# Re-planned tiles, banks and order of a two-branch kernel (head-wise linear attention beside an SSM convolution)

## The chip, the core and the metric

The kernel runs as one program on one core of a Trainium2 chip. The metric is the device time of one execution in microseconds (us). Engines are named as the profile names them: PE is TensorE (PEld its weight loads), DVE is VectorE, ACT is ScalarE, POOL is GpSimd, SP is SyncE, which here only issues DMAs.

## The reference

Two independent parts are computed and put side by side, 448 columns each, in bf16.

```python
# A: x 2048x448, 16 heads of 28
qkv = x @ wqkv
pq, pk = q @ w_phi, k @ w_phi                     # per head
phi = concat(softmax(p), softmax(-p))             # for q and for k
kv, z = phi_k^T v, sum of phi_k                   # per head
o = (phi_q kv) / (phi_q z + 1e-6);  a = o @ wo
# B: u 2048x448, 256 states for each column
dt = exp(log_dt)[:, None];  dA = dt * (A_re + 1j * A_im)
K[d, l] = real(sum_n C[d, n] * exp(dA[d, n] * l) * dt[d] * B[d, n])
b = causal_convolution(u, K) + u * Dskip
```

## The kernel before

**The A part.** x is loaded in four blocks of 512 rows and transposed on TensorE (`flip_x`, eight banks of transposes and eight evictions). `fold_weights` multiplies w_phi into the q and k weights. `key_side` runs over eight pairs of 128 tokens: projections, two Exp for each block (scale +1 and -1), a transposing DMA of the Exp tile on SP's queue (L600), matmuls with a 0/1 table that sum over heads, a reciprocal on VectorE (L187), the product VR and the key-value matmuls. `query_side` runs four times on 512 tokens: projection, Exp, a small normalisation on VectorE, a round trip through DRAM (SCd) that spreads it over partitions, two products, the output matmuls.

**The B part.** `to_states` turns A, B and C, which have the 448 columns on partitions, into tiles with 128 states on partitions (two halves of 256), by a matmul with a diagonal of dt; ScalarE's Exp and Sin then give the powers PW of exp(dA). The positions l, as bf16 holds them, are sums of a low position (48 rows) and a high one (16 rows). The 448 columns are done in four quarters (`qt`) of 112, each with 224 elements on each partition (112 columns, two state halves). For each quarter `rotations` (Sin), `dampings` (Exp), `damp` and `far` make the low table W, `hi_tables` the high table U, and `build_k` contracts both over the states with 448 small matmuls in 4 column groups. `scatter_k` rearranges K through DRAM. `signal_spectrum` and `kernel_spectrum` are matmuls with transform tables, `conv` multiplies the spectra on VectorE and transforms back (`inverse`), and stores.

**What sets the order.** No loop does. Each operation is recorded (`Prog.add`) and then issued in the order of the list ORDER, 1104 operations written out by hand or by a planner; each engine runs its own in that order, and waits for the others by semaphores. PSUM banks come from a second list, SLOTS. SBUF is one tile of 212,800 bytes on each partition, cut at offsets that are constants in the code (`oW`, `oT`, ...), some used twice. Copies are bound to an engine in the code: `acopy` (L193) on ScalarE, `vcopy` (L180) on VectorE, `smul` (L174) on VectorE; all other VectorE products and sums are L162, all Exp, Sin and Square are L190, all matmuls L201, transposes L211, all DMAs L216.

**Around the change.** u is loaded twice: even rows with 896-byte runs on SP (`rep_rows`), odd rows in reverse order, one row of 896 bytes for each partition and step, on POOL (`pair_rows`); VectorE then forms sum and difference (`ab`). The raw A, B and C tiles are loaded with 512-byte runs, `(j p) n -> p j n`. POOL issues 22 DMAs: eight of u, four of w_phi, the head mask, Dskip, wo, the head-sum table, the two halves of the inverse table GI, and the four SUd tiles of the convolutions. In ORDER, five of the eight key pairs stand ahead of `damp` of quarter 0.

Of the kernel before, what the change touches and what calls it, by code (L numbers as in the profile page):

```python
# [15 lines left out]

D_MODEL = 448
D_HEAD = 28
# [28 lines left out]
def _dft_tables():  # L47
# [24 lines left out]
    pid = np.zeros((128, 9, 128))  # L72
    for i, p in enumerate(ODD + [-1]):
        pid[np.arange(128), i, np.arange(128)] = p
    hm = np.zeros((112, 4, D_HEAD + 1))
# [7 lines left out]
class Prog:  # L83


    def __init__(self):
        self.ops = []
        self.jobs = []

    def take(self, kind, *slots):  # L90
        self.jobs.append((kind, slots, len(self.ops)))
        return SLOTS[len(self.jobs) - 1] if SLOTS else slots
# [13 lines left out]
def kernel(  # L106
# [26 lines left out]
    sbuf = sb_pool.tile([128, 212800 // 2], BF16, name="sbuf")  # L133
# [4 lines left out]
    def sb(off, shape, dtype=BF16):  # L138
        size = int(np.prod(shape[1:])) * (4 if dtype == F32 else 2)
        v = sbuf[0:shape[0], off // 2:(off + size) // 2]  # L140
        if dtype == F32:
            v = v.bitcast(F32)
        names = "abcdefg"[:len(shape) - 1]
        if len(names) > 1:
            v = v.rearrange(f"p ({' '.join(names)}) -> p {' '.join(names)}",
                            **{n: s for n, s in zip(names[1:], shape[2:])})
        return v
# [25 lines left out]
    def smul(o, a, s):  # L173
        prog.add("V", lambda: nc.vector.tensor_scalar_mul(o, a, s))  # L174

# [3 lines left out]
    def vcopy(o, a):  # L179
        prog.add("V", lambda: nc.vector.tensor_copy(o, a))  # L180

    def low(fn):
        with nc.allow_low_precision(reason="bf16 softmax weights, as in the reference"):
            fn()

    def recip(o, a):
        prog.add("V", lambda: low(lambda: nc.vector.reciprocal(o, a)))  # L187
# [4 lines left out]
    def acopy(o, a):  # L192
        prog.add("A", lambda: nc.scalar.copy(o, a))  # L193
# [20 lines left out]
    def dma(eng, o, i):  # L214
        e = {"S": nc.sync, "AD": nc.scalar, "G": nc.gpsimd}[eng]
        prog.add(eng, lambda: e.dma_start(out=o, in_=i))  # L216

    oCB, oAT, oTH, oPW, oW, oT, oU, oTM, oSQ, oTS, oKT, oX = (
        3584, 7168, 10752, 14336, 95104, 32256, 46592, 75264, 82432, 86912, 92400, 139008)
    PID = sb(0, [128, 9, 128])  # L220
    ident = PID[:, 0, :]
    NEG = PID[:, 8, :]
    DSK = sb(2304, [128, D_MODEL])
    HM = sb(3200, [112, 4, D_HEAD + 1])
    K0 = sb(86016, [128, D_MODEL])
    bias_hp = sb(3440, [128, 1], F32)
    KVZ = sb(3456, [112, 2, 4, 4, 2])
    CB = sb(oCB, [128, 2, NCOL])
    AT = sb(oAT, [128, 2, NCOL])
    TH = sb(oTH, [128, 2, NCOL])  # L230
    PW = {k: sb(oPW + 3584 * i, [128, 2, NCOL]) for i, k in enumerate((32, 64, 128, 256, 512))}
    W = sb(oW, [128, 2, N_LO, QC])
    T = sb(oT, [128, 2, 16, QC])
    U = [sb(oU + 14336 * b, [128, N_HI, 2, QC]) for b in range(2)]
    TS = [sb(oTS + 2744 * b, [128, N_LO, 28]) for b in range(2)]
    KT = [sb(oKT + 1344 * b, [128, N_KT, 112]) for b in range(2)]
# [3 lines left out]
    xT = sb(oX, [112, 4, 2048])  # L240
    Wp = [sb(o, [112, 4, D_MODEL]) for o in (155392, 158976)]
    WV = sb(162560, [112, 4, D_MODEL])
    M = sb(158976, [112, 8, D_MODEL])
    wo = sb(166144, [112, 4, D_MODEL])
    G1 = sb(169728, [128, 2, 4, 512])
    raw = {nm: sb(oT + 2048 * i, [112, 4, SSM_N]) for i, nm in enumerate(("Are", "Aim", "Cre", "Bre", "Cim", "Bim"))}
    srcs = {"Are": B_A_re, "Aim": B_A_im, "Cre": B_C_re, "Bre": B_B_re, "Cim": B_C_im, "Bim": B_B_im}
    XS = [sb(o, [128, 4, D_MODEL]) for o in (oW + 10976, oW + 14560, oW + 18144, oW + 32928)]
    Wqk = sb(oW + 36512, [112, 4, 2 * D_MODEL])
    wT = sb(oTS, [112, 2, 4, D_MODEL])  # L250
    BD = sb(oTS + 7168, [112, 4, 112])
    DG = sb(oSQ + 1024, [112, 4, 112])
    DGN = sb(oSQ + 1920, [112, 4, 112])
    ldt = sb(oSQ + 2816, [4, 112])
    dtr = sb(oSQ + 3072, [4, 112])

    def load_raw(nm):
        dma("S", raw[nm], srcs[nm].rearrange("(j p) n -> p j n", p=112))
# [4 lines left out]
    wq3 = A_wqkv.rearrange("(j p) n -> p j n", p=112)  # L263
    dma("S", ldt, bass.AP(tensor=B_log_dt.tensor, offset=B_log_dt.offset, ap=[[112, 4], [1, 112]]))
    load_raw("Are")
    dma("S", PID, P_d)
    load_raw("Aim")
    load_x(0)
    for nm in ("Cre", "Bre", "Cim", "Bim"):
        load_raw(nm)  # L270
    for i in range(1, 4):
        load_x(i)
    dma("S", Wqk, wq3[:, :, 0:2 * D_MODEL])
    mset(BD, 0.0)
    for hh in range(4):
        dma("G", BD[28 * hh:28 * hh + 28, :, 28 * hh:28 * hh + 28], A_w_phi.rearrange("(c h) d f -> h d c f", h=4)[hh])
    prog.add("V", lambda: nc.vector.memset(bias_hp, PI / 2))

    def rep_rows(row, a):
        rs = u2.ap[0][0]  # L280
        return bass.AP(tensor=u2.tensor, offset=u2[row + 128 * (1 - a), 0].offset,
                       ap=[[2 * rs, 64], [256 * rs, 4], [1, D_MODEL]])

    def pair_rows(row, t):
        rs = u2.ap[0][0]
        return bass.AP(tensor=u2.tensor, offset=u2[row + 1023 - 128 - 256 * t, 0].offset,
                       ap=[[128 * rs, 2], [-2 * rs, 64], [1, D_MODEL]])

    ua = [sb(o, [128, 4, 2, D_MODEL]) for o in (oU, oW + 10976)]
    ab = [sb(o, [128, 2, 4, D_MODEL]) for o in (198336, oU + 14336)]  # L290

    def load_u(b):
        for a in range(2):
            dma("S", ua[b][64 * a:64 * a + 64, :, 0, :], rep_rows(1024 * b, a))
        for t in range(4):
            dma("G", ua[b][:, t, 1, :], pair_rows(1024 * b, t))

    load_u(0)
    dma("S", G1, G_d)
    dma("S", WV, wq3[:, :, 2 * D_MODEL:])  # L300

    af(dtr, ldt, ACT.Exp)
    (b_,) = prog.take("P", 6)
    dtp = bank16(b_, [112, 4])
    transposes([(dtp, dtr, PID[0:4, 0, 0:4])])
    mul(DG, PID[0:112, 0, 0:112].unsqueeze(1).to_broadcast([112, 4, 112]), dtp.unsqueeze(2).to_broadcast([112, 4, 112]))
    smul(DGN, DG, -1.0)
# [4 lines left out]
    def halves(v):  # L312
        return v.rearrange("p (b x) -> p b x", b=2)

    def to_states(bs, terms):
        items = []
        for j in range(4):
            for nch in range(2):
                at = (j % 2) * QC + nch * 56
                o = view(psum[:, bs[j // 2], at:at + 1], [112, 2], [14, 4], [1, 14])  # L320
                items += acc(o, [(t[:, j, 128 * nch:128 * nch + 128],
                                  d[:, j, :].rearrange("p (g c q) -> p c g q", c=2, q=14)) for t, d in terms])
        mms(items)

    bA, bT = prog.take("P", 0, 1), prog.take("P", 4, 5)
    for nm, b, dst in (("Are", bA, AT), ("Aim", bT, TH)):
        to_states(b, [(raw[nm], DG)])
        acopy(halves(dst[:, 0, :]), two(b))
        sub(halves(dst[:, 1, :]), two(b), halves(dst[:, 0, :]))
    prog.take("T", 0)  # L330
    prods = {}
    for i, (a, b) in enumerate((("Cre", "Bre"), ("Cim", "Bim"), ("Cre", "Bim"), ("Cim", "Bre"))):
        prods[a + b] = sb(oTM + 2048 * i, [112, 4, SSM_N])
# [3 lines left out]
    amp = [sb(o, [128, NCOL], F32) for o in (oW, oW + 3584, oW + 7168, oW + 21952)]  # L337
    cs = [sb(o, [128, 2, NCOL], F32) for o in (oW + 25536, oU + 7168)]
    qa = [sb(oU + 14336 + 7168 * i, [128, 2, NCOL], F32) for i in range(2)]
    s2 = sb(177920, [128, 2, NCOL], F32)  # L340
    CR = sb(166144, [128, 2, NCOL])
    PW[16] = sb(194752, [128, 2, NCOL])
    for n, k in enumerate(LOWP):
        af(halves(amp[n]), two(bA), ACT.Exp, scale=float(k))
    for part, terms in enumerate(([("CreBre", DG), ("CimBim", DGN)], [("CreBim", DG), ("CimBre", DG)])):
        bs = prog.take("P", *((6, 7), (2, 3))[part])
        to_states(bs, [(prods[n], d) for n, d in terms])
        acopy(halves(CR[:, part, :]), two(bs))
    ones = sb(186944, [128, 128])
    mset(ones, 2.0 ** -17)  # L350
    bs = prog.take("P", 0)
    mms([it for qt in range(4) for it in acc(
        view(psum[:, bs[0], 112 * qt:112 * qt + 1], [28, 4], [14, 2], [1, 14]),
        [(ones, view(CR[:, 0, QC * qt + 56 * nch:QC * qt + 56 * nch + 1], [14, 4], [112, 2], [1, 14]))
         for nch in range(2)])])
    acopy(K0, psum[:, bs[0], 0:D_MODEL])
    for n, k in enumerate(LOWP):
        c_ = cs[n % 2]
        af(halves(c_[:, 0, :]), two(bT), ACT.Sin, scale=float(k), bias=bias_hp)
        af(halves(c_[:, 1, :]), two(bT), ACT.Sin, scale=float(k))  # L360
        mul(PW[k] if k != 128 else qa[0], c_, amp[n].unsqueeze(1).to_broadcast([128, 2, NCOL]))
        if k == 128:
            acopy(PW[128], qa[0])
    cur = qa[0]
    for i, k in enumerate((256, 512)):
        af(s2, cur, ACT.Square)
        nxt = qa[(i + 1) % 2]
        sub(nxt[:, 0, :], s2[:, 0, :], s2[:, 1, :])
        stt(nxt[:, 1, :], cur[:, 0, :], 2.0, cur[:, 1, :], ALU.mult, ALU.mult)
        acopy(PW[k], nxt)  # L370
        cur = nxt
    prog.take("T", 0)
    TM = sb(oTM, [128, 2, 2, NCOL])
# [3 lines left out]

    def flip_x(i):
        for tp in range(2):
            p = bank16(*prog.take("P", 6 + tp), [112, 2, 4, 128])  # L380
# [541 lines left out]
```

## Time and profile before

| | us |
|---|---|
| median of 3 runs (lowest, highest) | 298.96 (296.89, 300.54) |
| span of the profiled execution, the only time it has | 299.6 |
| busy: DVE, PE, ACT, PEld, POOL | 244.4, 240.7, 203.4, 179.8, 16.0 |
| table loads of ACT | 13 of 1.28 each |
| bytes moved | 39.47 MB in 65,966 packets, mean 132 GB/s |
| mean granted clock of PE | 0.949 |

The page's busy times are unions: two instructions of an engine that overlap count once. A row of the table of groups gives the count, the busy time and the mean of one instruction, then the engine's idle time just before such instructions and what ended it. In the 40 slices one digit is the busy share of 7.5 us in tenths.

### The profile page before, as it was taken

The page shows a single profiled execution, that of the slowest core. Times are in us where ns is not written, and L with a number is a line of the kernel's source. Part 1 is how long each engine was busy: PE and PEld are TensorE (multiplying, and loading weights), DVE is VectorE, ACT ScalarE, POOL GpSimd, SP SyncE. Part 2 cuts the span into 40 slices and gives each one's busy share as a digit, 9 for nine tenths or more (in the row PEclk, how much of TensorE's full clock was granted, in tenths as well). Part 3 has the DMA queues.
Part 4 walks back from the last instruction along what each step waited for, and adds up shares of the span by engine and source line. Part 5 has one row for each costly group of instructions (what it writes and reads, how often), then busy time and mean ns, then how long its engine had stood idle before and what let it go on. Part 6 is the DMA issues. An engine that isn't in the chain of part 4 may idle for free. (4 is left out here: it accounts for less than half of the span.)

```text
span 299.6 us, 8829 instructions
## 1 busy us (share of the span) xinstructions
PE 240.7 (80%) x3877; PEld 179.8 (60%) x3877; DVE 244.4 (82%) x292; ACT 203.4 (68%) x343; POOL 16.0 (5%) x32
## 2 busy tenths in 40 slices
PE   1246997899469999986979996566998888999784
PEld 1245554567245567863447763466658678999784
DVE  4265995446249999997989999989899999999991
ACT  3749999599947999997199955871948611544431
POOL 8102201001000000000000001000000000000000
PEclk9999999999959999998695999777999999999999
DMA  7999387463804530045012533955879956667222
GB/s 161 239 231 194 79 246 145 64 181 67 107 10 122 122 64 4 6 136 104 3 61 58 85 79 85 331 146 109 227 255 293 301 136 176 147 184 135 46 65 63
DMA packets 65966, 39.47 MB, mean 132 GB/s; under 512 B 46616, under 2 KB 61992, under 8 KB 65544
## 3 DMA queue, kind: packets, MB, share of 16 engines
q1 hardware_dynamic: 62920, 31.57, 45.0%
q0 software_dynamic: 3008, 7.34, 8.9%
q8 instruction: 30, 0.49, 0.7%
q14 instruction: 8, 0.07, 0.1%
HBM read 26.36 MB, written 8.85 MB: 118 GB/s over the span
## 5 line engine op out<-in xcount | busy, mean ns | idle before, releaser
L201 PE MATMUL psum<-sbuf 128*16 128x48 bf16 (+9 forms) x3768 | 231.3, 258 | 39.1 <-DVE sbuf L162 11.1
L201 PEld LDWEIGHTS <-sbuf 128*16 128x16 bf16 (+4 forms) x3768 | 170.7, 109 | 98.3 <-issue 37.3
L162 DVE TENSOR_TENSOR sbuf<-sbuf 128x896 bf16<-128x896 bf16 (+13 forms) x227 | 216.7, 1002 | 12.1 <-DMA sbuf<-SCd 3.5
L193 ACT CAST sbuf<-psum 128x448 bf16<-128x448 f32 (+4 forms) x141 | 74.9, 581 | 70.6 <-PE psum L201 63.1
L190 ACT ACTIVATE sbuf<-psum 128x448 bf16<-128x448 f32 (+4 forms) x140 | 81.7, 674 | 13.2 <-DVE sbuf L162 7.5
L211 PE MATMUL psum<-sbuf 128*112 128x128 bf16 (+3 forms) x109 | 11.7, 267 | 16.2 <-DMA sbuf<-in_A_x_dram 7.2
L190 ACT ACTIVATE sbuf<-psum,sbuf 128x896 bf16<-128x896 f32 (+3 forms) x28 | 21.7, 812 | 0.0
L211 PEld LDWEIGHTS <-sbuf 128*112 128x112 bf16 (+3 forms) x109 | 10.0, 172 | 17.8 <-DMA sbuf<-in_A_x_dram 7.7
L187 DVE RECIPROCAL sbuf<-psum 128x64 bf16<-128x64 f32 x8 | 4.4, 555 | 19.4 <-PE psum L201 19.4
L190 ACT ACT_TABLE_LOAD x13 | 16.7, 1283 | 0.9 <-PEq L906 0.7
L190 ACT ACTIVATE sbuf<-sbuf 128x896 bf16<-128x896 bf16 (+3 forms) x13 | 11.6, 915 | 3.6 <-DVE sbuf L162 3.4
L180 DVE COPY sbuf<-psum 112x1024 bf16<-112x1024 bf16 (+2 forms) x16 | 7.3, 466 | 7.8 <-PE psum L211 6.6
L216 POOL DMA_DIRECT2D sbuf<-const x4 | 2.2, 556 | 126.0 <-PE psum L201 109.5
L162 DVE TENSOR_TENSOR sbuf<-psum,sbuf 128x128 f32<-128x128 f32 (+3 forms) x10 | 4.7, 491 | 3.8 <-ACT sbuf L193 3.8
L193 ACT COPY sbuf<-psum 112x896 bf16<-112x896 bf16 x5 | 4.5, 919 | 4.7 <-PE psum L211 4.7
L216 POOL DMA_DIRECT2D sbuf<-in_B_u_dram x8 | 6.6, 830 | 19.0 <-DMA sbuf<-in_B_B_re_dram 18.9
L174 DVE TENSOR_SCALAR sbuf<-sbuf 128x3584 bf16<-128x3584 bf16 (+4 forms) x11 | 6.5, 587 | 0.0
L216 POOL DMA_DIRECT2D sbuf<-SUd x4 | 2.1, 529 | 72.5 <-DVE sbuf L162 72.5
L193 ACT CAST sbuf<-sbuf 128x1792 bf16<-128x1792 f32 x3 | 5.1, 1703 | 0.0
L180 DVE COPY sbuf<-sbuf 128x448 bf16<-128x448 bf16 (+1 forms) x6 | 1.4, 238 | 3.1 <-DMA sbuf<-const 3.1
L177 DVE SCALAR_TENSOR_TENSOR sbuf<-sbuf 128x64 f32<-128x64 f32 (+1 forms) x6 | 3.0, 506 | 0.0
L196 POOL MEMSET sbuf<- 128x32 bf16 (+3 forms) x6 | 1.4, 261 | 24.7 <-PE psum L211 24.5
(12 smaller groups left out, 9.4 us busy)
## 6 DMA issues: line engine op xcount, KB each, us to landing
sbuf<-const SPq DMA_DIRECT2D x16, 384.0 KB, 3.2
SUd<-sbuf SPq DMA_DIRECT2D x8, 448.0 KB, 4.3
sbuf<-SCd SPq DMA_DIRECT2D x16, 224.0 KB
sbuf<-SUd POOLq DMA_DIRECT2D x4, 896.0 KB, 4.9
sbuf<-const POOLq DMA_DIRECT2D x2, 1024.0 KB, 7.9
sbuf<-in_A_x_dram SPq DMA_DIRECT2D x4, 448.0 KB
out_dram<-sbuf SPq DMA_DIRECT2D x4, 448.0 KB
sbuf<-in_B_u_dram SPq DMA_DIRECT2D x16, 112.0 KB, 4.0
```

The costliest lines, as they stand in the source:

```text
L162: prog.add("V", lambda: nc.vector.tensor_tensor(out=o, in0=a, in1=b, op=op))
L174: prog.add("V", lambda: nc.vector.tensor_scalar_mul(o, a, s))
L177: prog.add("V", lambda: nc.vector.scalar_tensor_tensor(out=o, in0=a, scalar=s, in1=b, op0=op0, op1=op1))
L180: prog.add("V", lambda: nc.vector.tensor_copy(o, a))
L187: prog.add("V", lambda: low(lambda: nc.vector.reciprocal(o, a)))
L190: prog.add("A", lambda: nc.scalar.activation(o, a, fn, **kw))
L193: prog.add("A", lambda: nc.scalar.copy(o, a))
L196: prog.add("G", lambda: nc.gpsimd.memset(o, v))
L201: nc.tensor.matmul(o, lhsT=l, rhs=r, **kw)
L211: nc.tensor.transpose(o, i, idn)
L216: prog.add(eng, lambda: e.dma_start(out=o, in_=i))
```

## The change

It records the same operations with other helpers, and replaces all lists.

- SBUF offsets come from a list PLACES, so that each tile has an offset of its own and no name shares one by code; `cs`, `qa`, the low-table scratch, the transposed key tile and the output tiles are separate tiles now.
- Banks (SLOTS) and the order (ORDER, 1108 operations) are new. `damp` of quarter 0 stands ahead of all reciprocals of the key side.
- A third list, PICKS, names the engine of each copy, of each scaling by a constant and of each square: A (ScalarE) or V (VectorE).
- The raw tiles are loaded with four rows for each partition (2 KB runs); `to_states` writes PSUM with a step of two words, and its readers reorder.
- The u rows are loaded in pairs, 1792-byte runs; the odd rows are reversed by a matmul with a reversed identity, evicted to `ur`, and then added and subtracted.
- The damping table has three rows for each power, the third being the negated one, so the scaling no longer writes into W.
- The two last subtractions of `finish` become one of 896 elements; the constant 1 that `spectrum_terms` took from W has a tile of its own.
- All DMAs are issued by SP; dt comes as a column from the load, without a transpose.

```diff
-    def take(self, kind, *slots):
-        self.jobs.append((kind, slots, len(self.ops)))
-        return SLOTS[len(self.jobs) - 1] if SLOTS else slots
+    def banks(self, n):
+    def place(self):
+        self.bufs += 1
+        return PLACES[self.bufs - 1]
+    def pick(self):
...
+    def either(on_act, on_dve):
+        eng = prog.pick()
+        prog.add(eng, {"A": on_act, "V": on_dve}[eng])
+    def copy(o, a):
+        either(lambda: nc.scalar.copy(o, a), lambda: nc.vector.tensor_copy(o, a))
+    def scaled(o, a, s):
+        either(lambda: nc.scalar.activation(o, a, ACT.Copy, scale=s), lambda: nc.vector.tensor_scalar_mul(o, a, s))
...
-        dma("S", raw[nm], srcs[nm].rearrange("(j p) n -> p j n", p=112))
+        dma("S", raw[nm], srcs[nm].rearrange("(p j) n -> p j n", j=4))
...
-                at = (j % 2) * QC + nch * 56
-                o = view(psum[:, bs[j // 2], at:at + 1], [112, 2], [14, 4], [1, 14])
+                at = (j % 2) * 56 + j // 2
+                o = view(psum[:, bs[nch], at:at + 1], [112, 4], [14, 4], [2, 7])
...
     def signal_spectrum(b):
-        add(ab[b][:, 0], ua[b][:, :, 0, :], ua[b][:, :, 1, :])
-        sub(ab[b][:, 1], ua[b][:, :, 0, :], ua[b][:, :, 1, :])
+        for tp in range(2):
+            bs = prog.banks(2)
+            mms([(psum[:, bs[k], 0:D_MODEL], REV, ua[b][:, 3 - 2 * tp - k, 1, :], dict(start=True, stop=True))
+                 for k in range(2)])
+            copy(ur[:, 2 * tp:2 * tp + 2, :], two(bs))
+        add(ab[:, 0], ua[b][:, :, 0, :], ur)
+        sub(ab[:, 1], ua[b][:, :, 0, :], ur)
...
-        smul(W[:, 1, 0:31:2, x0:x0 + w], A[:, 0:31:2, x0:x0 + w], -1.0)
+        scaled(A[:, 2:48:3, x0:x0 + w], A[:, 0:46:3, x0:x0 + w], -1.0)
...
-            acopy(TS[qt % 2][:, :, x0:x0 + 7], psum[:, b, 0:7 * N_LO].rearrange("p (c l) -> p l c", c=7))
+            x0 = 14 * hq + c
+            copy(view(TS[:, 0, x0:x0 + 1], [28, N_LO], [2, 7]),
+                 psum[:, b, 0:7 * N_LO].rearrange("p (c l) -> p l c", c=7))
...
-            sub(S[:, 1, 0], y[:, 0, 0:448], y[:, 0, 448:896])
-            sub(S[:, 1, 1], y[:, 1, 448:896], y[:, 1, 0:448])
+            sub(S[:, 1], view(y[:, 0, 0:1], [1344, 2], [1, 448]), view(y[:, 0, 448:449], [448, 2], [1, 448]))
...
-        dma("G", SU.rearrange("p b c s m x -> p (b c s m x)"), SUd[qt].rearrange("p i x -> p (i x)"))
+        dma("S", SU.rearrange("p b c s m x -> p (b c s m x)"), SUd[qt].rearrange("p i x -> p (i x)"))
```

## The prediction

> **What bounds the kernel now.** I read the page's busy times and slices first, then busy time by stage, then VectorE's timeline, then the waits.
>
> ```profile
> span 299.6 us, 8829 instructions
> ...
> PE 240.7 (80%) x3877; PEld 179.8 (60%) x3877; DVE 244.4 (82%) x292; ACT 203.4 (68%) x343; POOL 16.0 (5%) x32
> ...
> DVE  4265995446249999997989999989899999999991
> ACT  3749999599947999997199955871948611544431
> ```
>
> VectorE (DVE) has the most work, 244.4 of 299.6 us, and its slices show where the other 55.2 us lie: nearly all before slice 13 (some 90 us). The busy times by stage, split at VectorE's first step of table 0 (87.9) and at its last result (292.3):
>
> ```profile
> 0.00:87.90 87.90, 58.92 (x507) 39.41 (x508) 48.10 (x57) 70.27 (x98) 12.87 (x26) 0.97 0.70 147
> 87.90:292.30 204.40, 178.04 (x3300) 136.81 (x3297) 195.72 (x235) 132.09 (x243) 3.18 (x6) 0.94 0.49 128
> 292.30:299.60 7.30, 3.71 (x72) 3.56 (x72) 0.57 (x2) 1.06 (x2) 0.00 (x0) 1.00 0.30 65
> ```
>
> The columns are the stretch, its length, PE, weight loads, DVE, ACT, POOL (busy us), granted clock, DMA share, GB/s. Stage A leaves VectorE idle for 87.9 - 48.1 = 39.8 us, stage B for 204.4 - 195.7 = 8.7, the tail for 6.7 of 7.3. In stage A it is ScalarE (ACT) that is full, 70.3 of 87.9. VectorE's timeline shows for what it waits there:
>
> ```profile
> 53.88 0.56 DVE L187 RECIPROCAL sbuf<-psum 128x64 bf16<-128x64 f32 x1 [4.70 <-PE psum L201]
> ...
> 60.49 0.56 DVE L187 RECIPROCAL sbuf<-psum 128x64 bf16<-128x64 f32 x1 [3.15 <-PE psum L201]
> ...
> 67.88 0.56 DVE L187 RECIPROCAL sbuf<-psum 128x64 bf16<-128x64 f32 x1 [2.71 <-PE psum L201]
> ...
> 85.22 0.56 DVE L187 RECIPROCAL sbuf<-psum 128x64 bf16<-128x64 f32 x1 [8.38 <-PE psum L201]
> ...
> 87.93 1.08 DVE L174 TENSOR_SCALAR sbuf<-sbuf 128x3584 bf16<-128x3584 bf16 x1
> ```
>
> These are four of the key side's eight reciprocals, one per pair of token blocks; between them VectorE has nothing queued that is ready. From 48.9 to 87.9 it works 15.2 of 39.0 us. Then the low table of quarter 0 starts, and from there VectorE is 96% busy. So the end is set by VectorE: what it has left when table 0 starts, some idle time, and the tail. Of the waits of SP's queue one line matters below (total, times, longest):
>
> ```profile
> SPq L216 <- ACT sbuf L193: 79.6, 21, 16.4
> ```
>
> **The change part by part.** Most rows' instructions overlap: count times mean over all rows gives 260.4 us for DVE and 237.3 for ACT, against 244.4 and 203.4 busy. I scale sums of row means by 0.939 and 0.857.
>
> *VectorE's work.* Counting both programs by form, VectorE gains 9 evictions of 448 (0.62 each, from the PSUM products of 112x448), 4 of 896 (1.087, from 128x896 out of PSUM), 2 of 112x896 (0.6, from 112x1024 at 0.678), one of 224 (0.4), three f32 to bf16 copies of 1792 and 2 squares of 896 (0.619): 5.6 + 4.3 + 1.2 + 0.4 + 4.5 + 1.2. The copies have no row; 0.62 (a bf16 scaling of that size) and 2.015 (an f32 product) bound them, and I take 1.5, nearer the f32 row since the source is f32. It loses 4 transposed-x evictions (2.7), 6 small ones (1.5), seven scalings (4.3) and two copies (0.5), and 16 subtractions of 448 become 8 of 896 (6.1 - 5.0 = 1.2). Net 17.2 - 10.2 = +7.0, scaled +6.7: 251.1. Bounds +4 and +8.
>
> *ScalarE's work.* It loses 3 table loads (13 to 10, 1.28 each), 3 f32 copies (1.70), 9 evictions of 448 (0.548) and a few more, together 17.9; it gains 2 scalings of 3584 and 2 of 1792, 4 transposed-x evictions, 6 small ones and some scalings, together 19.3 (the 3584 has no row; twice the 1792's 1.74 is the near one, four times 0.915 the high one). About +1: no relief. *TensorE* gains 8 reversals of 448 columns at 0.203 (26.0 us for 128), 1.6 us, on the early path of the u spectrum, beside x transposes that wait for DMA anyway; without that cover, 1.6 us at most.
>
> So no engine is relieved. A gain can only come from VectorE's idle time.
>
> *Stage A, the main step.* In the changed order 52 VectorE instructions stand ahead of the first product of table 0 (against 57 here): the five reciprocals and VR products of the key side that stand ahead here come behind it with the other three, most of high table 0 and both u sums stay ahead. By their rows these 52 are 50.8 us, scaled 47.7. The product waits for table 0's last Exp on ScalarE, its 62nd instruction: 54.2 us by rows, scaled 46.4, plus idle time at the head (here 4.8 us before the first Exp at 6.41, then 1.2, 0.9 and 4.5); with Are loaded first and Wqk no longer awaited by the first evictions I take 6.5, so about 53. VectorE itself idles at the head: here 15.7 us up to 28.1 (waits on PID, the A evictions, x, head mask and u). The x and mask waits fall, those for PID and Are stay; I take 10, bounds 5 and 15.7. So 47.7 + 10 = 58 us, later than ScalarE's 53, and stage A ends at 58 (53 to 63). VectorE then has 251.1 - 47.7 = 203.4 us left.
>
> *The DMAs.* The six raw loads go from 512-byte to 2 KB runs, the u loads from 896 to 1792 bytes and 12 issues to 4, and POOL's other 14 issues join SP. Through 30 us the DMA share is about 1.0 at some 200 GB/s, and G1 lets the first spectrum matmul go at 29.2. G1 stands behind 5.2 MB in the new queue, against 3.4 here, so at 200 GB/s it is there at 31 us; I cost that at nothing, since ScalarE reaches the first such eviction after 35 us of its own rows (scaled 30, plus 6.5); a G1 later than 35 would move stage A by the same amount. The four w_phi loads now stand behind a store of SUd on SP; the key weights' fold comes some 10 us later than that.
>
> *Stage B.* By the order TensorE has done 320 matmuls when stage A ends: 112 of 448 columns at 0.203 and 24 at 0.221, 56 transposes at 0.109, 56 of 112, 32 of 224, 40 of 112x112, together 46 us. 242.3 - 46 leaves 196, of which 194 in stage B. VectorE needs 203.4. With the idle time of today (8.7) the stage would be 212; with TensorE's idle time of today (204.4 - 178.0 = 26.4) 194 + 26.4 = 220, that is 17.6 of VectorE's. From 90 to 110 us here DVE ran 19.87 of 20 us beside PE 19.66 and ACT 17.98, so dense packing is possible. But between the first products of tables 0 and 1 VectorE has 57 us of work by rows, TensorE 58 and ScalarE 47: as dense, for far longer. I take 15, near the upper end: 218.4.
>
> *The tail.* Here 72 matmuls (3.71) follow the last subtraction. In the new order the first half of them stands before it, so 1.86 goes: 7.3 to 5.9, say 6; bounds 5.5 and 7.3.
>
> Sum: 58 + 203.4 + 15 + 6 = 282.4 us, against the profiled execution's 299.6, which stands 0.6 above the median of 298.96: 282. Bounds: 53 + 201 + 8.7 + 5.5 = 268 and 63 + 205 + 25 + 7.3 = 300.
>
> *A page's rule against the change.* The 48 state matmuls took 4.0 us, 83 ns each, writing PSUM in runs of 14 words; the new ones write every second word. The Trainium skill's "PSUM — Partial Sum Buffer", Specifications (TRN2), says that a non-contiguous access pattern slows matmuls significantly. If each doubled, by that rule, 4 us would come on top in the head, where TensorE waits 5.7 and 3.6 us for DMA: 282 to 286 if none of it were hidden. No run here shows the step of two.
>
> *A page's rule on the bound.* In stage B matmuls fill 87% and weight loads 67% (136.8 of 204.4). The Trainium skill's "Perfetto Trace Analysis", Identifying the Most-Contended Engine, says that matmul busy time is a poor measure of how near TensorE is to its limit and weight-load busy time a good one. By it TensorE has room, the idle time stays at 8.7 and the sum is 276.
>
> **The rivals.** *TensorE becomes the bound of stage B.* It keeps its present 87%: 194 / 0.871 = 223, and 58 + 223 + 6 = 287. For it: 194 us of work in 218. Against it: the dense stretch above. Still faster.
>
> *The idle time only moves.* The key side's chain (Exp, transposing DMA, sum matmuls, reciprocal) is not shortened, only put behind table 0. Its eight reciprocals still stand in VectorE's order ahead of table 1, and its DMAs take 3.9 us to landing each. If VectorE waits there as now between 48.9 and 87.9 (23.9 us, of which I have 6 in my 15), the time is 282 + 18 = 300: the same. Against it: the projections now run before table 0 ends, and each pair has its own transposed tile.
>
> *SP's queue holds everything (slower).* SP here waits 79.6 us in 21 waits for ScalarE's evictions, the longest 16.4, and now carries 14 more issues, among them the SUd and inverse-table loads that the convolutions need. Place: a load of the convolutions, or a transpose, behind a store whose eviction is late; VectorE's in-order queue stands with it. The price is the wait: two like the longest make 282 + 33 = 315. It decides from 23 us on, where 282 passes 305.
>
> **How the numbers follow.** About 2% is what a measurement tells from no change: under 293 is faster, over 305 slower. My case (269 to 290) has 0.46, TensorE as the bound 0.15, idle time that moves 0.19, SP's queue 0.20. The first two and a little of the third give faster 0.62, the rest of the third same 0.18, the last slower 0.20. The likeliest gives 282 us; the range 270 to 304 leaves out the slower rival and little else. The likeliest case's own range is 269 to 290.
>
> **What would show it.** Right: the first 128x6720 product of VectorE starts at 53 to 63 us, with some 10 us idle before it; the reciprocals come behind it; VectorE's busy time is 248 to 253; stage B's idle time is 9 to 18; 10 table loads. Wrong: a reciprocal with over 10 us of idle time before it, or VectorE waiting on a DMA from SUd; a first product after 70 us; f32 copies near 2 us each; TensorE's waits for evictions longer than now.

## The result, and the profile after

The changed kernel takes 308.66 us (median of 4 runs, 306.29 to 312.26), the kernel before beside it 299.75: a ratio of 1.030 (95% interval 1.021 to 1.039). It is slower, where 282 us were predicted. All ratios here are formed from undisturbed runs, so a median beside one can lie a little off it. The profiled execution took 307.84 us. From its page, in the columns of the one before:

```profile
span 306.1 us, 8839 instructions
...
PE 244.3 (80%) x3884; PEld 184.2 (60%) x3884; DVE 245.2 (80%) x286; ACT 204.3 (67%) x342; POOL 3.7 (1%) x23
...
DVE  3259869597997959999798179993997897999991
ACT  1675955986999439997776699977944614444331
```

VectorE works 245.2 us, 0.8 more than before, and ScalarE 0.9 more. The loss is idle time: VectorE idles 306.1 - 245.2 = 60.9 us, where it idled 55.2. The busy times by stage, split at VectorE's first 128x6720 product of table 0 and at its last subtraction (stretch, length, PE, PEld, DVE, ACT, POOL, granted clock, DMA share, GB/s):

```profile
0.00:70.92 70.92, 44.62 (x288) 29.61 (x289) 46.76 (x53) 47.84 (x63) 1.57 (x11) 0.95 0.49 129
70.92:299.30 228.38, 196.40 (x3534) 151.53 (x3534) 197.79 (x232) 155.88 (x279) 2.10 (x12) 0.92 0.54 130
299.30:306.10 6.80, 3.26 (x67) 3.09 (x63) 0.65 (x2) 0.53 (x1) 0.00 (x0) 1.00 0.42 90
```

VectorE idles 70.92 - 46.76 = 24.2 us in stage A (10 predicted) and 228.38 - 197.79 = 30.6 in stage B (15 predicted). In stage A no engine is full any more: ScalarE works 47.8 of 70.9. They wait for each other. Five of VectorE's longer waits, from its timeline (start, duration, what ran, idle time before it and who ended it):

```profile
17.38 1.09 DVE L175 TENSOR_TENSOR sbuf<-psum,sbuf 128x896 bf16<-128x896 f32 x1 [6.63 <-ACT sbuf L196]
...
37.78 0.69 DVE L203 COPY sbuf<-psum 112x1024 bf16<-112x1024 bf16 x1 [1.39 <-ACT sbuf L196]
...
44.13 1.16 DVE L203 COPY sbuf<-psum 112x896 bf16<-112x896 bf16 x2 [2.52 <-ACT sbuf L196]
...
177.84 7.60 DVE L175 TENSOR_TENSOR sbuf<-sbuf 128x6720 bf16<-128x6720 bf16 x4 [8.34 <-PE psum L218]
...
211.68 0.23 DVE L203 COPY sbuf<-psum 128x128 bf16<-128x128 bf16 x1 [4.93 <-ACT sbuf L196]
```

Odd in the three copies: each evicts PSUM that a transpose on PE has filled, yet ScalarE releases it, with an Exp or Sin (L196) that has nothing to do with it. The copy at 37.78 reads bank 5, filled at 34.51; the Sin that releases it reads banks 0 and 7 (SLOTS gives this job "07"), and bank 5 lies between them. The first row is another case: TH is the tile of A's imaginary part times dt, held as a bf16 value (the high part) and what that leaves over (the low part). The subtraction that forms the low part needs only PE's sums (there at 10.5 us) and the copy of the high part. While it waits, ScalarE's timeline has:

```profile
10.98 0.90 ACT L203 CAST sbuf<-psum 128x896 bf16<-128x896 f32 x1
11.77 2.56 ACT L196 ACTIVATE sbuf<-psum 128x896 f32<-128x896 f32 x3
14.32 1.28 ACT L196 ACT_TABLE_LOAD   x1
15.62 1.73 ACT L196 ACTIVATE sbuf<-psum 128x896 f32<-128x896 f32 x2
```

The copy ends at 11.9. The subtraction starts only when the two Sins end (17.35), which read the same two banks and stand ahead of it in ORDER. PE stands behind the subtraction in turn: 6.25 us idle up to 18.52.

**Theory S (spans).** When the program is built, a view over two banks (first bank, stride, second bank) is taken to touch the banks between them. Work of other engines in those banks then waits for it in the written order. I resolved every wait of the built program to the instruction that it names and compared the addresses: 52 waits among PE, ACT and DVE name an instruction that shares no bank with the waiter and whose span covers it; the kernel before has none. In SLOTS 23 of 48 pairs are not neighbours; before, all 45 were. Of these waits 38 are between PE and ACT, and so they show in the list of waits: PE for ACT's functions (Exp, Sin), before (L201, L190) and after, as total, times, longest:

```profile
PE psum L201 <- ACT sbuf L190: 6.6, 7, 2.5
```

```profile
PE psum L218 <- ACT sbuf L196: 18.5, 16, 3.9
```

**Rivals.** *O (order)*: the engines' in-order queues simply have the wrong things ahead, as at 17.38; the banks do not matter. *C (rate)*: PE at its granted clock (0.82 from 132 to 200 us) sets the second half, and whatever is won ahead of it is given back.

### The profile page after: what moved, and what is told of

It is laid out like the page before. It is cut to its first block, busy times and chain, and to the rows that moved or that the text cites. A ratio compares the mean times of both kernels' runs of the same rounds, so it can differ in the third digit from the quotient of the medians.

```text
span 306.1 us, 8839 instructions
## 1 busy us (share of the span) xinstructions
PE 244.3 (80%) x3884; PEld 184.2 (60%) x3884; DVE 245.2 (80%) x286; ACT 204.3 (67%) x342; POOL 3.7 (1%) x23
## 5 line engine op out<-in xcount | busy, mean ns | idle before, releaser
L218 PE MATMUL psum<-sbuf 128*16 128x48 bf16 (+9 forms) x3776 | 237.7, 261 | 54.3 <-ACT sbuf L196 18.5
L218 PEld LDWEIGHTS <-sbuf 128*16 128x16 bf16 (+4 forms) x3776 | 176.6, 110 | 113.5 <-issue 66.1
L175 DVE TENSOR_TENSOR sbuf<-sbuf 128x896 bf16<-128x896 bf16 (+13 forms) x220 | 212.8, 1028 | 27.6 <-PE psum L218 8.3
L196 ACT ACTIVATE sbuf<-psum 128x896 bf16<-128x896 f32 (+4 forms) x140 | 82.2, 714 | 13.9 <-DVE sbuf L284 6.3
L196 ACT ACTIVATE sbuf<-psum,sbuf 128x896 bf16<-128x896 f32 (+3 forms) x28 | 22.1, 819 | 5.2 <-PE psum L218 4.0
L203 DVE CAST sbuf<-psum 128x448 bf16<-128x448 f32 (+2 forms) x14 | 10.1, 736 | 5.8 <-PE psum L218 5.8
L228 PE MATMUL psum<-sbuf 128*112 128x128 bf16 (+2 forms) x108 | 9.4, 239 | 3.9 <-ACT sbuf L196 1.9
L206 ACT ACTIVATE sbuf<-sbuf 128x3584 bf16<-128x3584 bf16 (+3 forms) x7 | 12.3, 1753 | 0.0
L228 PEld LDWEIGHTS <-sbuf 128*112 128x112 bf16 (+2 forms) x108 | 8.4, 151 | 4.7 <-issue 3.8
L203 ACT COPY sbuf<-psum 112x1024 bf16<-112x1024 bf16 (+3 forms) x13 | 8.4, 653 | 2.4 <-PE psum L228 1.3
L209 ACT ACTIVATE sbuf<-sbuf 128x896 bf16<-128x896 bf16 (+2 forms) x10 | 9.8, 995 | 0.0
```

Of the source, the lines that this page charges most:

```text
L175: prog.add("V", lambda: nc.vector.tensor_tensor(out=o, in0=a, in1=b, op=op))
L196: prog.add("A", lambda: nc.scalar.activation(o, a, fn, **kw))
L203: either(lambda: nc.scalar.copy(o, a), lambda: nc.vector.tensor_copy(o, a))
L206: either(lambda: nc.scalar.activation(o, a, ACT.Copy, scale=s), lambda: nc.vector.tensor_scalar_mul(o, a, s))
L209: either(lambda: nc.scalar.activation(o, a, ACT.Square), lambda: nc.vector.tensor_tensor(out=o, in0=a, in1=a, op=ALU.mult))
L218: nc.tensor.matmul(o, lhsT=l, rhs=r, **kw)
```

## The experiments

What theory S expects in us comes from the built order played through again, every instruction at its duration in the trace, with the waits in question taken out.

**Neighbouring banks for every pair.** SLOTS alone; 56 of 208 jobs get other banks, no two that live at once share one.

```diff
-    "01 23 67 67 6 0 1 1 5 6 2 0 1 6 2 35 12 45 34 04 12 67 23 04 56 12 04 3 4 01 02 15 12 67 67 24 47 67 04 35 04 "
+    "01 23 67 67 6 0 1 7 5 6 2 0 1 6 2 45 01 45 34 23 01 67 23 23 56 01 01 3 4 01 01 45 12 67 67 23 67 67 23 45 23 "
...
```

> The changed kernel with one edit: every piece of work that holds two PSUM banks gets two neighbouring ones (in the changed kernel 23 of its 48 pairs have other banks between them, in the kernel before none of 45); order, copies, buffers and DMAs stay. Theory S (spans): a view over two banks that are not neighbours is taken, when the waits are set, to touch the banks between too, so that work of another engine in those banks waits for it in the written order; 52 waits of the changed kernel have no other reason (VectorE's copy at 37.78 us reads bank 5 and is released by ScalarE's Exp on banks 0 and 7; ScalarE's 4.05 us wait at 169.75 us and PE's 3.2 us at 150.04 us are of this kind). With the spans gone and every instruction at its duration in the profile of the changed kernel, the first 128x6720 product comes at 62 to 65 us instead of 70.9 and the end some 20 us earlier: 288 us (283 to 297). Theory O (order): VectorE waits because its in-order queue has the wrong things ahead; the banks do not matter: 306 to 310. Theory C (rate): PE at its granted clock sets the second half, and waits that go come back later: not under 303.

Measured: 289.85 us, ratio 0.965 (0.958 to 0.972). The first product stands at 61.17. The same instructions in the same order lose 19 us and pass the kernel before. The copies that waited at 37.78 and 44.13 no longer wait, and PE's waits for ACT's functions, 18.5 us in the changed kernel, shrink:

```profile
35.67 0.68 DVE L203 COPY sbuf<-psum 112x1024 bf16<-112x1024 bf16 x1
...
38.80 1.14 DVE L203 COPY sbuf<-psum 112x896 bf16<-112x896 bf16 x2
```

```profile
PE psum L218 <- ACT sbuf L196: 5.6, 6, 2.3
```

So the order alone does not make the loss (O), and what is won is not given back (C). Two things changed with the pairs here: 33 jobs that were not spread got other banks too, so some real sharing of banks is new, and in the profiled executions the granted clock is 0.964 against 0.928 and TensorE's work 238.4 us against 244.3. The renaming below keeps all sharing as it was.

**The subtraction first.**

```diff
-    "0 3 1 2 4 27 28 30 5 312 33 48 8 31 21 41 7 34 9 40 43 42 59 6 52 39 13 35 29 37 ...
+    "0 3 1 2 4 27 28 30 5 312 33 48 8 31 21 41 7 34 35 9 40 43 42 59 6 52 39 13 29 37 ...
```

> The changed kernel with one edit in the order: the subtraction that forms the low part of TH stands right behind the copy of its high part, ahead of the three Exps and two Sins that it now waits behind (VectorE stands 6.63 us in front of it, PE 6.25 us behind it). Theory O: this is what the head lost; the first 128x6720 product comes 6 to 7 us earlier (64 to 65 us) and the end 5 to 7 us earlier: 302 (300 to 304). Theory S: the head gains the same 6, the end 4 to 6, because the spans behind it stay: 302 to 305, so this run alone does not tell S from O; it prices the one wait. Theory C: given back by 170 us, where PE builds table 1: 306 to 310.

Measured: ratio 1.0065 (0.9985 to 1.0144), against 1.030 of the changed kernel: 2.3%, some 7 us by the ratios. The medians, 306.08 of ten runs (299.92 to 308.20) and 308.66, differ by 2.6 us only, and in the profiled execution of 305.9 us the first product stands at 68.55, 2.4 us earlier and not the 6 to 7 that were expected. So the 6.63 us wait goes (the subtraction starts at 11.46), but what that is worth beside the spread pairs stays uncertain; the next run prices it better. It is an order matter, which O has right, and the smaller part of the loss.

**Both.**

> Both edits together: neighbouring banks for every pair, and the subtraction of TH's low part ahead of the Exps and Sins. Theory S: the two are separate waits and add up: first 128x6720 product at 56 to 59 us (what the prediction had for the change itself), end 26 us under the changed kernel: 282 (277 to 292), under the kernel before too. Theory O: as the order edit alone, 300 to 304. Theory C: not under 303.

Measured: 284.96 us, ratio 0.951 (0.945 to 0.957): 24 us under the changed kernel, 15 under the kernel before. Against neighbouring banks alone the subtraction brings 4.9 us (289.85 to 284.96), and the first product 4.1 (61.17 to 57.05). The subtraction now waits for the copy of the high part:

```profile
11.99 1.09 DVE L175 TENSOR_TENSOR sbuf<-psum,sbuf 128x896 bf16<-128x896 f32 x1 [1.77 <-ACT sbuf L203]
```

The stages of this kernel, split in the same way:

```profile
0.00:57.05 57.05, 42.37 (x288) 28.73 (x289) 46.44 (x54) 46.86 (x63) 1.57 (x11) 1.00 0.61 161
57.05:276.60 219.55, 193.34 (x3534) 150.46 (x3534) 197.49 (x232) 156.63 (x279) 2.08 (x12) 0.94 0.57 135
276.60:283.30 6.70, 3.22 (x66) 3.05 (x63) 0.62 (x1) 0.53 (x1) 0.00 (x0) 0.97 0.47 100
```

Stage A has the length that the prediction gave the change: 57.05 us with 10.6 idle (58 with 10). What ends it is another engine than forecast: VectorE's last wait there, 0.87 us, is for ScalarE's Exps, which the prediction had done by 53. Stage B is 219.6 us, where 218.4 was forecast, but this agreement is luck: VectorE works 197.5 us in it and not 203.4, and idles 22.1 and not 15.

**The spread put into the kernel before.** One renaming of its banks (b to 3b mod 8), and as a control another that keeps neighbours (b to 7 - b):

```diff
-    "6 12 56 0 12 56 1 0 4 3 1 2 6 2 0 7 3 1 01 34 34 ...
+    "2 36 27 0 36 27 3 0 4 1 3 6 2 6 0 5 1 3 03 14 14 ...
```

> The kernel before with its bank numbers renamed one for one (0 1 2 3 4 5 6 7 become 0 3 6 1 4 7 2 5), nothing else: every pair of neighbours becomes a pair three or five banks apart, and whatever shared or did not share a bank before still does. Theory S: waits on the banks between appear that the kernel before does not have, and it becomes slower by more than the change made it: 320 to 340 us. Theories O and C: the banks' numbers do not matter: 297 to 302.

> A control for the renaming: the kernel before with its bank numbers renamed one for one from 0..7 to 7..0. Every bank has another number, and every pair of neighbours is still one. Theory S: no new wait, 297 to 302 us, the same as the kernel before. If any renaming cost time (what the 340.6 us of the spread renaming could also mean), it would be well over 305.

Measured: spread 340.58 us, ratio 1.138 (1.130 to 1.146); mirrored 1.003 (0.999 to 1.007). A renaming alone costs nothing, spread pairs cost 40 us, just above what was expected. By the same count the spread program has 81 waits on banks in between, the mirrored one none. VectorE's and ScalarE's work hardly grows (245.4 us against 244.4, 207.1 against 203.4); the waits are longer. TensorE's work grows from 240.7 to 248.5 us: the granted clock is 0.905 to 0.919 in the five runs, where the kernel before beside it has 0.937 to 0.960. The spread brings this too; how much of the 40 us goes through the clock was not separated. The row of PE's waits for ACT, 6.6 before, is now:

```profile
PE psum L201 <- ACT sbuf L190: 28.6, 25, 3.9
```

**Where the 19 us lie.** SLOTS again, for the pairs of the head alone, then for the others alone.

> The changed kernel with neighbouring banks only for the 13 spread pairs of the head (u spectrum, weight folds, rotations and dampings of table 0, all first written before the first 128x6720 product ends its stage); the 10 spread pairs of the key matrix and of tables 2 and 3 stay spread. Theory S: the price of the spans lies where they stand. With the waits of the 13 gone and all durations as in the changed kernel's profile, the first 128x6720 product comes at 62 to 65 us (70.9 in the changed kernel) and the end 8 us earlier: 300 (297 to 303). Rival A (only the head counts, the later waits are covered): 288 to 292, as with all 23. Rival B (what the head gives is given back later): 306 to 309.

> The other half: neighbouring banks only for the 10 spread pairs of the key matrix and of tables 2 and 3; the 13 of the head stay spread. Theory S: head unchanged (first 128x6720 product at 69 to 71 us), VectorE's 8.3 us wait at 169.5 us shrinks since TensorE and ScalarE no longer hold each other up there, the end 11 to 12 us earlier: 297 (293 to 300); the two halves together make the 19 us of all 23. Rival A: 306 to 309. Rival B: 288 to 292.

Measured: the 13 of the head 0.9895 (0.982 to 0.997), 4.1% under the changed kernel, first product at 60.55; the last 10 0.998 (0.993 to 1.003), 3.2%, first product at 68.56. The two halves add up to 7.3%, all 23 gave 6.5%; the head is worth more, the rest less than expected. Neither is given back. Of the 8.34 us wait at 177.84 half stays with the last 10 cured, and with all the edits 3.86 us:

```profile
158.14 4.03 DVE L175 TENSOR_TENSOR sbuf<-sbuf 128x6720 bf16<-128x6720 bf16 x3 [3.86 <-PE psum L218]
```

This rest is a real one: the product writes W, which PE still reads for table 1. There is one W; a second was not tried.

**The copies that went to VectorE.** In the kernel with both edits, three letters of PICKS go from V to A.

> The kernel with both edits (neighbouring banks, subtraction first; 285.0 us), with the three f32 to bf16 copies of 1792 columns back on ScalarE as in the kernel before. If VectorE's work sets the end one for one, its 3.2 us less (three at 1.08) make 281 to 283. If in the head ScalarE is as late as VectorE (the first product there waits 0.87 us for ScalarE's Exps), three copies at 1.70 us put the first 128x6720 product from 57 to 61 or 62 us and the end to 290 (287 to 292).

Measured: 292.14 us, ratio 0.974 (0.966 to 0.982), 2.3% or 7 us above the base; first product at 62.63. From the groups by form, the kernel with both edits, then this one (busy, mean ns of one):

```profile
L203 DVE CAST sbuf<-sbuf 128x1792 bf16<-128x1792 f32 x3 | 3.3, 1085 | 0.0
```

```profile
L203 ACT CAST sbuf<-sbuf 128x1792 bf16<-128x1792 f32 x3 | 5.2, 1743 | 0.0
```

VectorE has 3.3 us less to do and the kernel is 7 us slower, because ScalarE's 5.2 us lie ahead of the Exps that the first product waits for; 5.6 of the 7 us are there when that product starts. Less work for the busiest engine is no gain where another one releases it.

**Short raw runs.**

```diff
-        dma("S", raw[nm], srcs[nm].rearrange("(p j) n -> p j n", j=4))
+        dma("S", raw[nm], srcs[nm].rearrange("(j p) n -> p j n", j=4))
```

> The kernel with both edits (285.0 us), with the six raw loads of A, B and C in 512-byte runs as in the kernel before, in place of 2 KB runs. Left out: the rows then stand on other partitions, so A, B and C meet the wrong dt, which changes no instruction. The prediction costed the longer runs at nothing. In the kernel before Aim landed at 9.9 us, issued at 2.05, against 5.8 in the changed one, issued at 2.13: if the head waits for it, TH's copy, its subtraction and all behind come some 3 us later: first product at 59 to 61, end 288 (286 to 291). If other work covers it: 284 to 286.

Measured: 286.05 us, ratio 0.9545 (0.949 to 0.960): not to be told from the base. The last parts of the eight first loads land between 0.5 us earlier and 0.2 us later, and the first product stands at 56.59. In the kernel before Aim was late for another reason than its runs; which, was not tried.

**Runs of 7 words.** `to_states` writes at `at = (j % 2) * 56 + 7 * (j // 2)` with `[1, 7]`; K0's sum and build_k's copy to TS (`x0 = 2 * hq + c`, step 4) follow.

> The kernel with both edits (285.0 us, 0.951 of the kernel before), with the 48 state matmuls writing PSUM in runs of 7 neighbouring words in place of every second word (the two halves of a group of 14 states stand one behind the other; the two places that read the group's order, K0's sum and the copies that scatter the kernel, get strides to match; K0's sum has 16 small matmuls in place of 8). These 48 matmuls took 4.0 us in the kernel before, in runs of 14 words, and 8.0 us in the changed one, 8.2 in the base here. If the step of two is what costs, as the prediction weighed it: 4 to 5 us for the 48, TH's subtraction at 11 us in place of 12.0, and the end 1 to 3 us earlier: 282 to 284, 0.94 to 0.947 of the kernel before. If it is the runs' shortness or the new order of the weights: 8 us still, and 284 to 287.

Measured: ratio 0.947 (0.939 to 0.956); the end cannot be told from the base (0.945 to 0.957). The matmuls can. The 48 in the kernel before, the changed one and this one (busy, mean ns):

```profile
L201 PE MATMUL psum<-sbuf 112*128 112x112 bf16 x48 | 4.0, 241 | 0.9 <-DMA sbuf<-in_B_A_re_dram 0.9
```

```profile
L218 PE MATMUL psum<-sbuf 112*128 112x112 bf16 x48 | 8.0, 411 | 7.4 <-DVE sbuf L175 7.4
```

```profile
L218 PE MATMUL psum<-sbuf 112*128 112x112 bf16 x48 | 5.5, 317 | 7.3 <-DVE sbuf L175 7.3
```

The first 16 took 3.14 us in the base and 1.86 here, the second 3.17 and 1.89, the third 1.85 and 1.79. The first product comes at 54.96, 2.1 us earlier.

## Why the prediction was wrong, point by point

- *VectorE's work, +6.7 (+4 to +8).* It was +0.8. The f32 copies took 1.083 us, not 1.5, which is 1.25 of it. Count times mean over all rows went from 260.4 to 265.1, +4.7 where I had +7.0, and more of it overlaps (245.2 / 265.1 = 0.925 against 0.939). That VectorE had 5.9 us less to do than forecast (245.2, not 251.1) hid part of the miss.
- *ScalarE about +1, 10 table loads.* Right: +0.9, and 10. TensorE's +1.6 was +3.6, at a clock of 0.928 against 0.949; with neighbouring banks it is 238.4, under the kernel before.
- *Stage A at 58 (53 to 63).* This is the step that failed: VectorE's idle time of 10 us and ScalarE's last Exp at 53. The idle time was 24.2 us, and the first product waited for that Exp until 70.92. I took head waits from the kernel before and counted ScalarE's work, but did not ask which instructions wait for which once the banks and the order were new. VectorE's 47.7 us of work was right (46.8). With the spread pairs and the one subtraction mended the stage ends at 57.05.
- *The DMAs at nothing.* Not contradicted. G1 landed at about 38 instead of 31, later than the 35 from which I had it move stage A; it did not, since the matmul that reads it starts at 48.8 and is released by ScalarE. Short raw runs change nothing. The longer u runs and the single queue were not tried alone.
- *Stage B, 15 us idle.* It was 30.6: the same step failed here. The stage is only 10.0 us longer than forecast, since VectorE's work in it was put 5.6 us too high. With the edits 22.1 stay idle: the terms left out there are W's single buffer (3.9) and VectorE's waits for projections and sums of the key side (3.7 and 3.4). The 17.6 that I drew from TensorE's idle time is 220.4 - 203.4 = 17.0, which does not touch the sum.
- *Tail 6.* 6.8, and 6.7 with the edits: inside the bounds, but not for my reason. Of the 72 matmuls 67 still follow the last subtraction (3.26 us), not half.
- *A page's rule against the change.* The Trainium skill's "PSUM — Partial Sum Buffer", Specifications (TRN2), says that a non-contiguous access pattern slows matmuls. The trace agrees for two groups of 16 (3.14 and 3.17 us, 1.86 and 1.89 in runs of 7), not for the third (1.85 and 1.79). The 48 took 4 us more of TensorE's time, as I had weighed it; with runs of 7 in place of the step 2.7 of it go (8.2 in the base, 5.5), about 2 us of stage A, and at the end nothing that can be told from the noise.
- *A page's rule on the bound.* The Trainium skill's "Perfetto Trace Analysis", Identifying the Most-Contended Engine, says to judge TensorE's headroom by the busy share of its weight loads. They fill 69% of stage B with the edits (150.46 of 219.55), matmuls 88%, and VectorE idles 22.1 us, not the 8.7 that I drew from it. The trace does not bear my conclusion out: some 13 of the 22.1 us are waits for TensorE.
- *Rivals.* Two of the three did not come: reciprocals wait 3.4 us in all, and no wait of VectorE on a load from SUd appears. TensorE as the bound is harder to judge. It fills 86% of the changed kernel's stage B (196.40 of 228.38), close to that rival's 87%, but neighbouring banks shorten the stage to 217.5 us with the same matmuls, so TensorE did not set it. With the edits it fills 88%, and there the rival is not excluded. The slower case that came was not on the list: waits that no data asks for, from the numbers of the banks. The list of signs had its marks, though: a first product after 70 us (70.92), and "TensorE's waits for evictions longer than now" (PE for ACT's copies 8.7 us against 5.1).

## What to carry to other kernels

In a diff, read lists of banks and buffers like code: a pair that an instruction reads as one view should be neighbours, or everything in the banks between lines up behind it. Resolve the waits of the built program to the instructions that they name; a wait between two that share neither data nor a bank is an order that the layout made, and it can be taken out without touching the work. And check where a reader of a bank stands in the order among readers on other engines, since they wait for each other as well.

## What the runs showed that was not expected

- Two engines that only read the same PSUM bank are put in a row by the built program: 17 such waits in the changed kernel, 30 in the kernel before. One held VectorE for 6.6 us and, with neighbouring banks, was worth 4.9 us of the end; what the others cost was not tried.
- Writing every second word of PSUM made the first 32 of the 48 state matmuls 1.7 times as long (3.14 against 1.86 us for 16), and left the last 16, which follow 2 us of uninterrupted transposes, as they were. Why the third group is spared was not settled.
